# Query and key weights in halves, and later stores and loads, in the attention loop of a four-layer kernel on one core

## The chip, the core and the metric

The kernel runs on one core of a Trainium2 chip. The metric is the device time of one execution in microseconds (us). The core has five engines with a queue of instructions each: TensorE (PE, whose weight loads are the row PEld), VectorE (DVE), ScalarE (ACT), GpSimd (POOL) and SyncE (SP). In this kernel nearly all transfers between the chip's memory and the core's are issued on SP's queue, in the order in which they are written there; an instruction of SP that waits holds back everything behind it.

## The reference

`x` is 2048 rows of 512 numbers. Four layers follow each other, A, B, A, B, each added to its own input after a layer norm; this text is about B.

```
x = x + A(layernorm(x)); x = x + B(layernorm(x)); x = x + A(...); x = x + B(...)

B:  q, k, v = x @ wq, x @ wk, x @ wv      # 32 heads of 16, four segments of 512 rows
    for s in range(4):                     # M, z: memory, starts at zero
        p = softmax(q_s k_s^T / 4 + causal mask);   a_dot = p @ v_s
        a_mem = (phi(q_s) @ M) / (phi(q_s) @ z + 1e-6)      # phi(t) = t + 1 if t > 0 else exp(t)
        o_s = g * a_mem + (1 - g) * a_dot                   # g = sigmoid(beta), one for each head
        M += phi(k_s)^T v_s;  z += sum(phi(k_s))
    return o @ wo
```

A is a linear attention with a learned feature map (two softmaxes for each head), computed in two passes over the rows.

## The kernel before

All matrix products are made from high and low parts, `hi*hi + hi*lo + lo*hi`, so a weight or an activation is a pair of tiles (`hh` and `hl` for the normed rows, `oh` and `ol` for the attention's output).

The attention loop (`LayerB.steps`) runs once for each B layer, through 160 steps `k` and some ahead of them. A *segment* is 40 steps, a *period* five: the period works on four heads (two row halves of a group of eight). Step `k` = 40s + 5m + j is written as the cell "m.j" of a table; `FIRST` is the table of segment 0, `GAPS` of segments 1 and 2, `LAST` (first loop) and `FINAL` (second loop) of segment 3. In each step the attention proper comes first (`attend`: matmuls into `lg`, ACT's exponential into `P`; `maxima`: matmuls into `mx`, `my` or `g`, DVE's maxima; in a period's first step also `weighted`). Then come the functions that earlier steps put off to this step (`self.at`), the copies of projected K and Q into the attention's operand tiles (`stack`, the transfers `e<-ta`, three in step 2 and three in step 4 of a period), and last what the step's cell names, which fills PE's row between the attention's matmuls.

The cells that matter here:

- `Q0+/6` to `Q3/6`: six steps of `proj_pair`, the projection of query (m = 0) and key (m = 1) for a group of eight heads. The weights of a group are 512 KB for each of the two (a tile `wqk` of 128 rows, 2 parts x 4 row blocks x 128 columns), read from memory.
- `V+/6`: six steps of the values' projection of the next segment. `O/6`: six steps of `out_pair`, the output projection of two tiles of 128 rows of the segment before. Pair 1 runs in the cells 2.1 to 2.4, pair 2 in 3.1 to 3.4 (in `FINAL`, two half-width pairs each, 2.1 to 5.4).
- `turn`: transposes the attention's output of one row tile and loads the residual rows (`mmq<-x`, `xr<-x`).
- `load`: loads the four row tiles for a later segment's norm (`x<-x`). `n` runs a piece of that norm at the next step.
- `begin` in segment 2 starts the next layer's rows.

A pair (`mm3_pair`) has 24 steps of two matmuls each, which use 64 of PE's 128 rows each and start together. Sides change rows twice. In steps 0 to 5 the first side (the query's, for a projection) takes its row blocks 0 and 1 on the upper rows and the second side on the lower; in steps 6 to 17 all four row blocks are taken with the sides exchanged; in steps 18 to 23 the blocks 2 and 3 as at first. Step 6 and step 18 must follow the matmuls before them, which is written as a *handover*: a no-op on SP that waits for PE's last matmul, and PE's next that waits for the no-op. So four cells hold a pair (0 to 5, 6 to 11, 12 to 17, 18 to 23), and its two handovers stand in SP's queue at the ends of the first and third cell.

The refill (`queue_w`) of a pair's weights is asked for when the pair has ended: two transfers of 512 KB, into the tile that the pair has just read, each waiting for the pair's last matmul. Q2 (cells 0.1 to 0.4) is followed by Q3 (1.1 to 1.4) after one step; the other projections are a period apart. The first two projections of a loop (`proj`, before step 0) are made singly, without handovers.

`out_pair` ends, for each of its two row tiles, with ACT's copy, POOL's addition of the residual and the store on SP (`x<-xr`, `x<-mmq`), one after the other.

Each transfer on SP's queue waits, beside its data, for the landing of the transfer eight places ahead of it, since eight semaphores are used in turn.

Of the kernel before, what the change touches and what calls it, by code (L numbers as in the profile page):

```python
# [8 lines left out]
F32R = mybir.dt.float32r  # L9
# [6 lines left out]
D = 512  # L16
H = 32
DH = 16
P = 128
NSEG = 4  # L20
NC = D // P
# [35 lines left out]
1.0 t0 fin max     | 1.1 Q3/6          | 1.2 Q3/6          | 1.3 Q3/6 | 1.4 Q3/6  # L57
2.0 m0 ln ln ln ln max fin | 2.1 V+/6     | 2.2 V+/6 w        | 2.3 V+/6 | 2.4 V+/6 w
3.0 t1 fin max     | 3.1 V+/6          | 3.2 V+/6 w        | 3.3 V+/6 | 3.4 V+/6 w
4.0 m1 max fin     | 4.1 Q0+/6 load    | 4.2 Q0+/6         | 4.3 Q0+/6 | 4.4 Q0+/6  # L60
5.0 t2 fin max     | 5.1 V+/6          | 5.2 V+/6 n        | 5.3 V+/6 n | 5.4 V+/6
6.0 m2 t3 fin max  | 6.1 Q1+/6         | 6.2 Q1+/6 n       | 6.3 Q1+/6 n | 6.4 Q1+/6
7.0 m3 a0+ a0+ max fin | 7.1 V+/6      | 7.2 V+/6 n        | 7.3 V+/6 n | 7.4 V+/6
# [3 lines left out]
1.0 t0 turn fin max | 1.1 Q3/6      | 1.2 Q3/6 n        | 1.3 Q3/6 | 1.4 Q3/6  # L67
2.0 m0 turn t1 fin ln max | 2.1 O/6    | 2.2 O/6           | 2.3 O/6 | 2.4 O/6
3.0 m1 turn turn fin ln max | 3.1 O/6  | 3.2 O/6           | 3.3 O/6 | 3.4 O/6
4.0 ln ln a2 fin a2 max | 4.1 Q0+/6 load | 4.2 Q0+/6       | 4.3 Q0+/6 | 4.4 Q0+/6  # L70
5.0 t2 a3 fin max  | 5.1 V+/6 begin  | 5.2 V+/6 n N      | 5.3 V+/6 n N | 5.4 V+/6
6.0 m2 a3 t3 fin max | 6.1 Q1+/6       | 6.2 Q1+/6 n N     | 6.3 Q1+/6 n N | 6.4 Q1+/6
7.0 m3 a0+ a0+ max fin | 7.1 V+/6      | 7.2 V+/6 n N      | 7.3 V+/6 n N | 7.4 V+/6
# [26 lines left out]
@with_exitstack  # L100
def interleave_kernel(ctx, tc, x_in, a_wqkv, a_wphi, a_wo, b_wq, b_wk, b_wv, b_wo, b_beta,
                      c_ident, c_mask, c_bd, out):
    nc = tc.nc
    MUL, ADD, SUB, MAX, MIN = ALU.mult, ALU.add, ALU.subtract, ALU.max, ALU.min

    cp = ctx.enter_context(tc.tile_pool(name="cp", bufs=1))
    wp = ctx.enter_context(tc.tile_pool(name="wp", bufs=4))
# [7 lines left out]
    def nm(s):  # L115
        uid[0] += 1
        return f"{s}_{uid[0]}"

    def T2(tag, bufs, dt=F32, shape=(P, 512)):
        return sp.tile(list(shape), dt, tag=tag, bufs=bufs, name=nm(tag))  # L120

    def PS(tag, bufs, shape=(P, 512)):
        return ps.tile(list(shape), F32, tag=tag, bufs=bufs, name=nm(tag))
# [38 lines left out]
    dve, act, pool, sync = [Ordered(e) for e in (nc.vector, nc.scalar, nc.gpsimd, nc.sync)]  # L162
# [10 lines left out]
    def mm(*a, **k):  # L173
        n = a[0].free_size()
        work[0] += n / 2.26 if k["rhs"].dtype == F32R else (n * 2 / 2.4 + 25 if "tile_position" in k else 2 * max(112, n * 2 / 2.4))
        return held(nc.tensor.matmul(*a, **k))  # L176
# [5 lines left out]
    def dma(out, in_):  # L182
        sync.dma_start(out=out.bitcast(F32), in_=in_.bitcast(F32))
# [35 lines left out]
    def dtile(shape, name):  # L219
        return dr.tile(list(shape), F32, name=name)  # L220
# [10 lines left out]
    def bring(w, key, src=None, tag="w8", low=dve):  # L231
        hi, lo = wtiles(tag)
        w[:] = [hi, lo]
        if key in kept:
            for kc in range(NC):
                for t, k in zip((hi, lo), kept[key]):
                    dma(t[:, kc, :], k[:, kc, :])
                yield
            return
        for kc in range(NC):  # L240
            raw = src(kc)
            act.copy(hi[:, kc, :], raw)
            low.tensor_tensor(out=lo[:, kc, :], in0=raw, in1=hi[:, kc, :].bitcast(F32), op=SUB)
            yield
        kept[key] = (dtile((P, NC, D), key + "_hi"), dtile((P, NC, D), key + "_lo"))
        owed.extend(zip(kept[key], (hi, lo)))
# [48 lines left out]
    wqk = [dtile((P, NC, 2, NC, P), f"wqk{m}") for m in range(2)]  # L295
# [137 lines left out]
    def mm3(po, lhs, rhs, kcs=range(NC)):  # L433

        for kc in kcs:
            for n, (a, b) in enumerate(((0, 0), (0, 1), (1, 0))):
                mm(po, lhsT=lhs(a, kc), rhs=rhs(b, kc), start=(kc == kcs[0] and n == 0),
                   stop=(kc == kcs[-1] and n == 2))
            if kc < kcs[-1]:
                yield  # L440

    def after(i, j):

        tc.add_manual_dep(i.ins, j.ins.name,
                          mybir.DependencyInfo(mybir.DependencyClass.Sync, mybir.DependencyReason.DATA),
                          reason="the halves of the rows take turns at a bank")

    def mm3_pair(one, two, kcs=range(NC)):

        terms = [(kc, a, b) for kc in kcs for a, b in ((0, 0), (0, 1), (1, 0))]  # L450
        half = len(terms) // 2
        parts = [(terms[:half], (one, two)), (terms, (two, one)), (terms[half:], (one, two))]
        steps = [(*term, sides, n == 0) for part, sides in parts for n, term in enumerate(part)]
        for step, (kc, a, b, sides, first) in enumerate(steps):
            ends = step == 0, step == len(steps) - 1
            for row, (po, lhs, rhs) in zip((0, 64), sides):
                i = mm(po, lhsT=lhs(a, kc)[row : row + 64], rhs=rhs(b, kc)[row : row + 64],
                       start=ends[0], stop=ends[1], tile_position=(row, 0))
                if first and step > 0 and row == 0:
                    after(i, passed)  # L460
            if step + 1 < len(steps) and steps[step + 1][4]:
                passed = sync.nop(nofuse=True)
                after(passed, i)
            if not ends[1]:
                yield
# [33 lines left out]
        wait(end)  # L499
        yield  # L500

    def out_pair(tiles, xdst, w, w0=0, w1=D):

        pos = [PS("g", G) for _ in tiles]

        def side(po, o):
            return (po[:, 0 : w1 - w0], lambda a, kc: o[a][:, kc * P : (kc + 1) * P],
                    lambda b, kc: w[b][:, kc, w0:w1])

        yield from mm3_pair(*[side(po, o) for po, (x, i, o) in zip(pos, tiles)])  # L510
        for po, (x, i, o) in zip(pos, tiles):
            y = T2("tb3", TB3)[:, 0 : w1 - w0]
            act.copy(y, po[:, 0 : w1 - w0])
            pool.tensor_tensor(out=x[:, w0:w1], in0=y, in1=x[:, w0:w1], op=ADD)
            if w1 == D:
                sync.dma_start(out=xdst[i], in_=x)
        yield

    def weigh(out, p, eps, add, eng=pool):
# [451 lines left out]
    class LayerB:  # L971
# [24 lines left out]
            yield from v_tile(self.hT[s], self.wv, self.vv[s], ("g", G), (0, 3, 1, 2) if s == 0 else range(4),  # L996
                              2 if s == 1 else s > 0)

        def queue_w(self):

            if self.wnext:
                m, c = self.wnext.pop(0)
                w = wp.tile([P, 2, NC, P], F32R, tag="w4", bufs=2, name=nm("wqk"))
                dma(w, wqk[m][:, c])
                self.w4.append(w)

        def proj(self, s, c, m):

            d, hT, w = self.st.setdefault((s, c), {}), self.hT[s], self.w4.pop(0)
            pp = PS("g", G)  # L1010
            yield from mm3(pp, lambda a, kc: w[:, a, kc, :], lambda b, kc: hT[b][:, kc, :])
            self.queue_w()
            for n, f in enumerate(self.projected(s, c, m, pp)):
                self.at.setdefault(self.k + 1 + n, []).append(f)
            yield

        def proj_pair(self, s, c):

            self.st.setdefault((s, c), {})
            hT, ws = self.hT[s], [self.w4.pop(0) for _ in range(2)]  # L1020
            pps = [PS("g", G) for _ in range(2)]

            def side(pp, w):
                return pp, lambda a, kc: w[:, a, kc, :], lambda b, kc: hT[b][:, kc, :]

            yield from mm3_pair(*[side(pp, w) for pp, w in zip(pps, ws)])
            jobs = []
            for m in range(2):
                self.queue_w()
                jobs.append(self.projected(s, c, m, pps[m]))  # L1030
            for m, job in enumerate(jobs):
                for n, f in zip((2, 4, 6) if m == 0 else (3, 5), job):
                    self.at.setdefault(self.k + n, []).append(f)
            yield
# [211 lines left out]
        def out(self, s):  # L1246
            for t in (0, 2):
                tiles = [(x, 4 * s + t + n, oT) for n, (oT, x) in enumerate(self.turned[0:2])]
                del self.turned[0:2]
                parts = 2 if self.thin and s == NSEG - 2 else 1  # L1250
                for n in range(parts):
                    yield from out_pair(tiles, self.xdst, self.wo, n * D // parts, (n + 1) * D // parts)

        def early(self):

# [37 lines left out]
                sync.dma_start(out=self.xdst[4 * s + t], in_=self.xe[t])  # L1293

        def opening(self):
            self.w4 = []
            self.wnext = [(m, c) for _ in range(NSEG) for c in range(NC) for m in range(2)]
            for _ in range(2):
                self.queue_w()
                yield  # L1300
            self.wv = []
            yield from bring(self.wv, "bwv")
            self.norm0 = self.norm(0)
            next(self.norm0)
            fills = self.start()
            for n in (0, 0, 1, 0, 1, 0, 1, 1, 1, 1, 0, 1, 1, 1, 1, 1, 1, 1, 1):
                yield
                next(self.norm0 if n else fills, None)
# [150 lines left out]
    for i in range(2):  # L1459
# [3 lines left out]
        a2 = la[i].pass2()  # L1463
# [40 lines left out]
```

## Time and profile before

| | us |
|---|---|
| median of 3 runs (lowest to highest) | 1428.81 (1425.95 to 1428.88) |
| the profiled execution | 1426.99 |
| its span, from the first to the last instruction | 1425.3 |

The profile is of one execution. A row of the timeline reads: start, duration, engine, line, operation, what it writes `<-` what it reads, shape, number of equal instructions merged, and in brackets how long the engine had been idle before and what ended that. Engines with a "q" are the queue that issues transfers: a row there is the time of issuing, not of the transfer. Buffer numbers are left out, so `x<-xr` is a store of a residual tile. L154 is the line of a helper that records every instruction of DVE, ACT, POOL and SP, and L176 that of all matmuls; groups are told apart by their tiles. The first attention loop lies between 303 and 720 us, the second between 997 and 1410.

### The profile page before, as it was taken

Reading aid. Unit: us, or ns where it says so; the run is one execution under the profiler, and the core shown is the slowest. Engines: PE = TensorE matmul, PEld = TensorE weight load, DVE = VectorE, ACT = ScalarE, POOL = GpSimd, SP = SyncE. Lnnn points to the kernel's source line nnn. Section 1 sums busy time; section 2 is a strip of 40 time slices with the busy share of each in tenths; the row PEclk is TensorE's granted clock in tenths of the full one; section 3 lists DMA queues with packets and bytes.
Section 4 is the critical chain, followed back from the end, with each engine's and each line's share of the span. In section 5 each row is a group of like instructions: output and inputs, shape, how many; then the busy total and the mean of one; then the engine's idle time right before and its main releaser. Section 6 shows DMA issues by size and latency. Waiting matters only on the chain.

```text
span 1425.3 us, 36885 instructions
## 1 busy us (share of the span) xinstructions
PE 1350.1 (95%) x14136; PEld 1035.5 (73%) x14136; DVE 1051.4 (74%) x3261; ACT 809.3 (57%) x1198; POOL 688.9 (48%) x1052
## 2 busy tenths in 40 slices
PE   7999989999999999999899998999999999999987
PEld 6887778767677777777568886887766777777765
DVE  4665778677787887888646767867678878878872
ACT  5545345436677677676534434453566766766663
POOL 1568656414447447335324446542335556554441
PEclk9999999999999999999999999999999999999998
DMA  5397346535545445456431104754464554544431
GB/s 195 109 328 273 115 154 207 171 99 151 144 124 134 132 126 140 128 131 168 143 104 45 60 31 131 249 167 122 128 186 98 138 154 98 135 129 96 113 104 46
DMA packets 108800, 196.27 MB, mean 138 GB/s; under 512 B 14416, under 2 KB 27856, under 8 KB 107856
## 3 DMA queue, kind: packets, MB, share of 16 engines
q1 hardware_dynamic: 106656, 193.27, 46.4%
q8 instruction: 112, 1.84, 0.6%
q10 hardware_dynamic: 1968, 0.64, 0.2%
q14 instruction: 64, 0.52, 0.1%
HBM read 101.05 MB, written 39.85 MB: 99 GB/s over the span
## 4 chain that ended last, share of the span: by engine, by line
PE 64%; DVE 14%; ACT 6%; DMA 6%; POOL 5%; issue 3%; SPq 2%; ACTq 0%; DVEq 0%; POOLq 0%
PE g L176 49%; PE lg L176 6%; PE g L180 4%; ACT P L154 3%; DMA wqk<-wqk 3%; PE mx L176 3%; POOL tb L154 2%; DVE es L154 2%; POOL P L154 2%; SPq L154 2%; DVE g L154 1%; DVE my L154 1%; PE lg L180 1%; DVE mx L154 1%; PE my L176 1%
## 5 line engine op out<-in xcount | busy, mean ns | idle before, releaser
L154 ACT ACTIVATE P<-lg 128x1024 f32<-128x1024 f32 x320 | 329.4, 1029 | 183.1 <-PE lg L176 94.3
L154 POOL TENSOR_SCALAR_AFFINE_SELECT P<-P 128x256 f32<-128x256 f32 (+1 forms) x448 | 192.4, 444 | 337.2 <-ACT P L154 336.5
L176 PE MATMUL g<-hh,wqk 64*128 64x512 f32 (+1 forms) x960 | 193.8, 393 | 7.7 <-DMA wqk<-wqk 5.4
L154 DVE CUSTOM_DVE_ANT_0 mx<-mx,mask 128x128 f32<-128x128 f32 (+3 forms) x332 | 165.2, 498 | 34.9 <-PE my L176 28.2
L154 DVE CUSTOM_DVE_ANT_0 g<-g,mask 128x512 f32<-128x512 f32 x360 | 176.0, 545 | 15.8 <-PE g L176 15.1
L176 PE MATMUL g<-w,oh 64*128 64x512 f32 (+2 forms) x816 | 174.8, 390 | 5.4 <-SPq L154 3.7
L154 DVE CUSTOM_DVE_ANT_0 my<-my,mask 128x128 f32<-128x128 f32 (+3 forms) x332 | 172.3, 519 | 0.1
L176 PE MATMUL lg<-e,e 64*128 64x256 f32 (+2 forms) x1024 | 157.3, 354 | 15.2 <-ACT P L154 14.7
L176 PE MATMUL g<-P,v 128*32 128x512 f32 (+3 forms) x2048 | 151.1, 435 | 4.4 <-DVE mxs L154 4.0
L176 PE MATMUL g<-w,hh 64*128 64x512 f32 (+2 forms) x800 | 147.8, 359 | 3.1 <-ACT w L154 1.3
L154 DVE DVE_READ_ACCUMULATOR2_ANT mxs<- 128x1 f32 x1024 | 144.7, 141 | 0.0
L176 PEld LDWEIGHTS lg<-e,e 64*128 64x128 f32 x1024 | 95.5, 186 | 63.5 <-ACT P L154 41.1
L176 PEld LDWEIGHTS g<-hh,wqk 64*128 64x128 f32 (+1 forms) x960 | 114.3, 185 | 25.3 <-issue 5.3
L176 PEld LDWEIGHTS g<-P,v 128*32 128x32 f32 x2048 | 59.8, 109 | 89.0 <-issue 64.9
L154 POOL TENSOR_SCALAR tb<-tb 128x512 f32<-128x512 f32 x72 | 110.9, 1551 | 25.4 <-ACT tb L154 25.4
L176 PEld LDWEIGHTS g<-w,oh 64*128 64x128 f32 (+1 forms) x816 | 100.5, 190 | 27.3 <-SPq L154 8.6
L176 PE MATMUL g<-hl,wqk 64*128 64x512 f32 (+1 forms) x480 | 113.8, 391 | 0.4 <-DVE hl L154 0.4
L176 PE MATMUL g<-w,ol 64*128 64x512 f32 (+2 forms) x408 | 108.7, 382 | 0.5 <-DVE ol L154 0.5
L176 PEld LDWEIGHTS g<-w,hh 64*128 64x128 f32 (+1 forms) x800 | 93.4, 188 | 17.0 <-ACT w L154 1.6
L176 PE MATMUL g<-w,hl 64*128 64x512 f32 (+2 forms) x400 | 94.7, 357 | 0.0
L154 ACT COPY tb<-g 128x512 f32<-128x512 f32 (+1 forms) x124 | 66.8, 575 | 43.5 <-PE g L176 43.3
L176 PE MATMUL mx<-e,e 63*128 63x256 f32 (+2 forms) x332 | 88.9, 330 | 0.3 <-DVE mxs L154 0.2
(149 smaller groups left out, 2882.4 us busy)
## 6 DMA issues: line engine op xcount, KB each, us to landing
e<-ta SPq DMA_DIRECT2D x384, 128.0 KB
wqk<-wqk SPq DMA_DIRECT2D x64, 512.0 KB
x<-x SPq DMA_DIRECT2D x48, 256.0 KB
ot<-in SPq DMA_DIRECT2D x28, 256.0 KB
pq<-tb SPq DMA_DIRECT2D x24, 256.0 KB
tb<-pq SPq DMA_DIRECT2D x24, 256.0 KB
x<-xr SPq DMA_DIRECT2D x22, 256.0 KB
xr<-x SPq DMA_DIRECT2D x20, 256.0 KB
```

Of the source, the lines that this page charges most:

```text
L154: i = f(*a, **k)
L176: return held(nc.tensor.matmul(*a, **k))
L180: return held(nc.tensor.transpose(*a))
```

## The change

Three things.

1. The two weight tiles are allocated once, and a refill is made in halves: row blocks 0 and 1, and row blocks 2 and 3, of both the query's and the key's weights (256 KB each, in runs of 1 KB instead of 4 KB). In a pair, the first halves are asked for after step 12 has been written and the second halves after the last step. Single projections and the opening ask for both halves, one after the other.
2. The stores of an out pair are put off: by five steps in segments 1 and 2, by two in segment 3. In cell 3.4 (4.4) they then come behind the second handover of the pair that follows.
3. `load` moves from cell 4.1, where it followed the pair's first six steps, to 4.4, ahead of the last six.

The order on PE, DVE, ACT and POOL stays; SP's changes, with 64 transfers more.

```diff
-4.0 m1 max fin     | 4.1 Q0+/6 load    | 4.2 Q0+/6         | 4.3 Q0+/6 | 4.4 Q0+/6
+4.0 m1 max fin     | 4.1 Q0+/6         | 4.2 Q0+/6         | 4.3 Q0+/6 | 4.4 load Q0+/6
...
-4.0 ln ln a2 fin a2 max | 4.1 Q0+/6 load | 4.2 Q0+/6       | 4.3 Q0+/6 | 4.4 Q0+/6
+4.0 ln ln a2 fin a2 max | 4.1 Q0+/6      | 4.2 Q0+/6       | 4.3 Q0+/6 | 4.4 load Q0+/6
...
-    def out_pair(tiles, xdst, w, w0=0, w1=D):
+    def out_pair(tiles, xdst, w, soon, w0=0, w1=D):
...
             if w1 == D:
-                sync.dma_start(out=xdst[i], in_=x)
+                soon(lambda x=x, i=i: sync.dma_start(out=xdst[i], in_=x))
...
-        def queue_w(self):
-
-            if self.wnext:
-                m, c = self.wnext.pop(0)
-                w = wp.tile([P, 2, NC, P], F32R, tag="w4", bufs=2, name=nm("wqk"))
-                dma(w, wqk[m][:, c])
-                self.w4.append(w)
+        def queue_w(self, m, halves=range(2)):
+
+            for half in halves:
+                if self.wnext[m][half]:
+                    c, kcs = self.wnext[m][half].pop(0), slice(2 * half, 2 * half + 2)
+                    dma(self.w4[m][:, :, kcs, :], wqk[m][:, c, :, kcs, :])
...
-            yield from mm3_pair(*[side(pp, w) for pp, w in zip(pps, ws)])
+            for n, _ in enumerate(mm3_pair(*[side(pp, w) for pp, w in zip(pps, ws)])):
+                if n == 12:
+                    for m in range(2):
+                        self.queue_w(m, (0,))
+                yield
             jobs = []
             for m in range(2):
-                self.queue_w()
+                self.queue_w(m, (1,))
                 jobs.append(self.projected(s, c, m, pps[m]))
...
-                    yield from out_pair(tiles, self.xdst, self.wo, n * D // parts, (n + 1) * D // parts)
+                    yield from out_pair(tiles, self.xdst, self.wo, lambda f: self.at.setdefault(self.k + (5 if s < NSEG - 2 else 2), []).append(f),
+                                        n * D // parts, (n + 1) * D // parts)
...
-            self.w4 = []
-            self.wnext = [(m, c) for _ in range(NSEG) for c in range(NC) for m in range(2)]
-            for _ in range(2):
-                self.queue_w()
+            self.w4 = [wp.tile([P, 2, NC, P], F32R, tag="w4", bufs=2, name=nm("wqk")) for _ in range(2)]
+            self.wnext = [[[c for _ in range(NSEG) for c in range(NC)] for _ in range(2)] for _ in range(2)]
+            for m in range(2):
+                self.queue_w(m)
                 yield
```

More of the change, by code (lines that the diff above doesn't have):

```diff
@@ L997, in values @@
                               2 if s == 1 else s > 0)
-        def queue_w(self):
-            if self.wnext:
-                m, c = self.wnext.pop(0)
-                w = wp.tile([P, 2, NC, P], F32R, tag="w4", bufs=2, name=nm("wqk"))
-                dma(w, wqk[m][:, c])
-                self.w4.append(w)
+        def queue_w(self, m, halves=range(2)):
[3 more added lines that the diff above has]
+                    dma(self.w4[m][:, :, kcs, :], wqk[m][:, c, :, kcs, :])
         def proj(self, s, c, m):
-            d, hT, w = self.st.setdefault((s, c), {}), self.hT[s], self.w4.pop(0)
+            d, hT, w = self.st.setdefault((s, c), {}), self.hT[s], self.w4[m]
             pp = PS("g", G)
             yield from mm3(pp, lambda a, kc: w[:, a, kc, :], lambda b, kc: hT[b][:, kc, :])
-            self.queue_w()
+            self.queue_w(m)
             for n, f in enumerate(self.projected(s, c, m, pp)):
@@ L1019, in proj_pair @@
             self.st.setdefault((s, c), {})
-            hT, ws = self.hT[s], [self.w4.pop(0) for _ in range(2)]
+            hT, ws = self.hT[s], self.w4
             pps = [PS("g", G) for _ in range(2)]
@@ L1295, in opening @@
         def opening(self):
-            self.w4 = []
-            self.wnext = [(m, c) for _ in range(NSEG) for c in range(NC) for m in range(2)]
-            for _ in range(2):
-                self.queue_w()
+            self.w4 = [wp.tile([P, 2, NC, P], F32R, tag="w4", bufs=2, name=nm("wqk")) for _ in range(2)]
+            self.wnext = [[[c for _ in range(NSEG) for c in range(NC)] for _ in range(2)] for _ in range(2)]
+            for m in range(2):
+                self.queue_w(m)
                 yield
```

## The prediction

> **What bounds the kernel now.** I read the page first, then the waits of PE, then the timeline around the waits that the diff can touch.
>
> ```profile
> span 1425.3 us, 36885 instructions
> ...
> PE 1350.1 (95%) x14136; PEld 1035.5 (73%) x14136; DVE 1051.4 (74%) x3261; ACT 809.3 (57%) x1198; POOL 688.9 (48%) x1052
> ...
> PE 64%; DVE 14%; ACT 6%; DMA 6%; POOL 5%; issue 3%; SPq 2%; ACTq 0%; DVEq 0%; POOLq 0%
> ```
>
> PE is busy for 1350.1 of 1425.3 us and carries 64% of the chain that ended last. PE runs its instructions in one written order, which the change leaves as it is (only SP's order and the waits differ in the built program), so a gain is a gap in PE's row that closes, and a loss is one that opens. The waits, listed by who waited for whom (total us, times, longest), name the gaps:
>
> ```profile
> PE lg L176 <- ACT P L154: 14.7, 57, 0.6
> ...
> PE g L176 <- DMA wqk<-wqk: 5.4, 10, 0.8
> ...
> PE g L176 <- SPq L154: 4.4, 6, 1.1
> ```
>
> The second row is what the split refill is about, the third what the moved stores and loads are about: a handover goes through a no-op on SP's queue, so whatever SP is stuck on ahead of it holds PE.
>
> **The refill, as it is.** In segment 1 of the first attention loop SP issues both refills when the pair Q2 has ended; the chain of waits runs through the second:
>
> ```profile
> 418.69 1.01 SPq L154 DMA_DIRECT2D wqk<-wqk  x2
> ```
>
> ```profile
> 419.31 5.12 DMA wqk<-wqk
> ```
>
> Q3's first two matmuls, by PE's timeline:
>
> ```profile
> 423.41 0.39 PE L176 MATMUL g<-hh,wqk 64*128 64x512 f32 x1
> 424.57 0.47 PE L176 MATMUL g<-hh,wqk 64*128 64x512 f32 x1 [0.78 <-DMA wqk<-wqk]
> ```
>
> The query side's weights are there at 423.41, the key side's only at 424.4; the two matmuls of a step otherwise start together (x2 rows below). From start to start 1.16 us are lost, though the gap between the records is 0.78, because the first matmul's record runs 0.39 us and would have been overlapped. Where the first matmul of the pair is the one that waits, the surplus is smaller:
>
> ```profile
> 529.26 0.34 PE L176 MATMUL my<-e,e 63*128 63x384 f32 x1
> 529.87 0.47 PE L176 MATMUL g<-hh,wqk 64*128 64x512 f32 x1 [0.27 <-DMA wqk<-wqk]
> ...
> 470.62 0.33 PE L176 MATMUL my<-e,e 63*128 63x384 f32 x1
> 470.79 0.40 PE L176 MATMUL g<-hh,wqk 64*128 64x512 f32 x2
> 471.03 0.40 PE L176 MATMUL g<-hl,wqk 64*128 64x512 f32 x2
> ```
>
> That is 0.61 from start to start against 0.17 at an undisturbed place: 0.44 lost, 0.17 over the gap. Records overlap where PE runs undisturbed, so a stall has to be measured between starts: ten waits of 5.4 us in all cost 5.4 + 10 x 0.3 = 8.4 us (7.1 with 0.17 each, 9.2 with 0.38). [...]
>
> **What the halves do to it.** Half 0 (row blocks 0 and 1 of both weights) is queued after a pair's thirteenth step, when the last reader, step 11, may have ended; half 1 after the pair. Step 11's last matmuls, the thirteenth step and the nineteenth, which waits for the second handover, stand in the pair Q0+ of the same segment at 469.84, 470.79 (above) and 472.65:
>
> ```profile
> 466.60 0.54 PE L176 MATMUL g<-hh,wqk 64*128 64x512 f32 x2
> ...
> 469.84 0.40 PE L176 MATMUL g<-hh,wqk 64*128 64x512 f32 x2
> ...
> 472.65 0.40 PE L176 MATMUL g<-hh,wqk 64*128 64x512 f32 x2
> ```
>
> ```profile
> 474.53 1.05 SPq L154 DMA_DIRECT2D wqk<-wqk  x2
> ```
>
> Step 11 ends at 470.24, 4.3 us ahead of that pair's own refill. Q2's refill is issued at 418.69, so its half 0 can be issued near 414.4 and is due at 423.4, 9 us later; the whole 1 MB took 5.12 us, so half of it is there. Half 1 is issued at 418.7 as now and due at Q3's thirteenth step, 4.2 us (470.79 less 466.60, the pair's first step) after 423.4, thus 8.9 us again. Both fit, so the 8.4 us go and nothing of the refill comes last. Runs in the weights' rows shrink from 4 KB to 1 KB, bytes stay; should halves move at half the rate, 512 KB still need what 1 MB needs now, 5.12.
>
> **The stores, as they are.** The first out pair's stores wait for POOL's additions, which wait for ACT's copies; the next pair's residual loads and first handover stand behind them:
>
> ```profile
> 451.92 0.33 SPq L154 DMA_DIRECT2D x<-xr  x1
> 453.17 0.33 SPq L154 DMA_DIRECT2D x<-mmq  x1
> 453.54 0.43 SPq L154 DMA_DIRECT2D mmq<-x  x1
> 454.01 0.46 SPq L154 DMA_DIRECT2D xr<-x  x1
> ```
>
> ```profile
> 453.33 0.40 PE L176 MATMUL g<-e,e 63*128 63x512 f32 x2
> 454.87 0.73 PE L176 MATMUL g<-w,oh 64*128 64x512 f32 x4 [1.14 <-SPq L154]
> ...
> 561.11 0.50 PE L176 MATMUL g<-w,oh 64*128 64x512 f32 x2 [0.84 <-SPq L154]
> ...
> 1148.71 0.51 PE L176 MATMUL g<-w,oh 64*128 64x512 f32 x2 [0.86 <-SPq L154]
> ...
> 1255.29 0.50 PE L176 MATMUL g<-w,oh 64*128 64x512 f32 x2 [0.84 <-SPq L154]
> ```
>
> SP is free of the last load at 454.47 and PE goes on at 454.87. The four waits are 3.7 us by gaps; the start-to-start surplus is about 0.16 each (453.33 to 454.87 is 1.54, against the 0.24 that two such matmuls of 512 columns take, 470.79 to 471.03), so 4.3 us. With the stores five steps later, behind the second handover, the loads can be issued as soon as SP gets there, and the 4.3 go. The stores of the last out pairs move by two steps only, still ahead of a handover, where no row of PE shows a wait for SP now: nothing.
>
> **The next rows' loads.** Four loads at cell 4.1 hold the K and Q pieces and then the second handover of Q0+:
>
> ```profile
> 1162.25 2.46 SPq L154 DMA_DIRECT2D x<-x  x4
> ```
>
> ```profile
> 1166.70 0.50 PE L176 MATMUL g<-hh,wqk 64*128 64x512 f32 x2 [0.17 <-SPq L154]
> ```
>
> One such gap, 0.2 us. At 4.4 they stand ahead of the second halves, which are due a period later; their own reader (the first moments, at 5.3) comes four steps after, so nothing is lost there.
>
> **What it adds.** 64 more issues on SP:
>
> ```profile
> L154 SPq DMA_DIRECT2D wqk<-wqk x64: 319/405/656, 167.0 to 1325.2; - x64
> ...
> L154 SPq DMA_DIRECT2D wqk<-ta x16: 513/567/1448, 49.6 to 114.8; - x16
> ```
>
> Of these, 52 are inside pairs: 13 pairs in each loop have a first half to fetch, two issues each (16 head groups, less two projected singly and the last, with nothing to fetch). Two issues from 470.24 (step 11's end) take 0.8 us at the median, 1.1 at the 567 ns of the pieces with short runs, and the handover behind them is needed at 472.65: hidden, 2.4 us of cover. The other 12 (opening and single projections) lie in the second pass, where POOL sometimes waits for loads:
>
> ```profile
> POOL P L154 <- DMA tb<-pq: 11.9, 6, 2.8
> ```
>
> Between nothing and 12 x 0.405 = 4.9 us; SP mostly stands waiting there, so 0.6.
>
> **What stays of the gain.** Sum of the gaps: 8.4 + 4.3 + 0.2 = 12.9. Once PE is earlier, other engines can come last. Two rows of the windows view bound that (span, then PE, PEld, DVE, ACT, POOL busy, clock, DMA):
>
> ```profile
> 513.20:525.50 12.30, 12.30 (x133) 9.32 (x128) 10.31 (x42) 9.03 (x13) 8.90 (x17) 1.00 0.31 66
> 525.50:539.60 14.10, 13.05 (x133) 10.05 (x127) 10.24 (x38) 10.52 (x18) 5.73 (x10) 1.00 0.61 164
> ```
>
> ```profile
> ACT P L154 <- PE lg L176: 94.3, 121, 3.1
> ```
>
> The first stretch is Q2's period, the second Q3's, with two refill waits. Q2's runs in 12.3 us with DVE at 10.3; Q3's has 10.2 of DVE and 10.5 of ACT, so 12.3 to 12.4 is possible for it: all kept. Against that, ACT's lead where it stood waiting for PE is 94.3/121 = 0.78 us, less than the 1.16 that PE gains at a time: 0.78/1.16 = 67% kept. I take 80%: 10.3, less 0.6: 9.7 us. The profiled execution took 1426.99 around its span of 1425.3, so it would take 1417.3; the median of the runs is 1.8 above it, and 1428.8 - 9.7 = 1419.1.
>
> **Rivals.** (a) Part of it only. The residual loads (453.54, 454.01) may still come late ahead of the first handover, leaving 0.8 x 8.6 - 0.6 = 6.3 us, 1422.5; or the K pieces, now queued behind half 0 and the stores, come late for the maxima:
>
> ```profile
> 472.45 1.99 SPq L154 DMA_DIRECT2D e<-ta  x3
> ...
> 478.82 0.28 PE L176 MATMUL mx<-e,e 63*128 63x256 f32 x1
> ```
>
> With half 0 and the two stores, 1 MB, in front of them, counted from the K pieces' issue, near 473.1 by then, 5.12 us for it and 1.9 for their own 384 KB, they land at 480.1, 1.3 late, in four places: 5.2 us, and 1424.3 is left. Against it: half 0 is issued from 470.24 on, two microseconds before the stores. [...] (b) Nothing to measure: ACT's exponentials come last wherever PE is early; the 14.7 us of waits for them grow by what the others lose, about 1427. For it stands that 57 waits are there already, against it Q2's period. (c) Slower: the second handover comes late, because SP must issue two halves between step 11 and it. The cover is 2.4 us, so it decides from 1.2 us an issue, and outweighs the gain from (2.4 + 9.7/26)/2 = 1.39 us; at the 1.45 us of the slowest short-run piece above, 26 x 0.5 = 13 us come in, 1428.8 - 9.7 + 13 = 1432. The medians, 0.41 and 0.57, speak against it. (d) The halves are not independent, and PE waits at mid-pair for the half just asked for: 26 x 2.6 us (half of 5.12), 1493 with the stores' share of the gain. The built order shows the thirteenth step waiting for the earlier half alone, so I leave it at 1 in 100.
>
> **Chances.** Forecast 0.60, (a) 0.17, (b) 0.08, (c) 0.14, (d) 0.01. Some 0.2% (2.9 us) is what a measurement here tells from no change. Faster 0.77, same 0.08, slower 0.15. The range runs from all 12.9 kept and half of the 2.9 us between the lowest and the highest of the three runs (1414.4) to case (b), 1427.0.
>
> **What would show it.** Right: no wait of PE for the refill or, in the out pairs, for SP; the stretch from one Q2 to the next pair's end near 12.4; the half-0 issues ending before 472. Wrong: SPq gaps at the nineteenth step of pairs (c); the maxima waiting for K pieces at 5.1 (a); more and longer waits of PE for ACT's exponentials (b); a DMA gap at the thirteenth step (d).

## The result, and the profile after

| us | before | changed |
|---|---|---|
| median (lowest to highest), first measurement | 1428.85 (1425.95 to 1429.28), 4 runs | 1412.97 (1411.68 to 1415.26), 4 runs |
| ratio | | 0.9898 [0.9880, 0.9917] |
| median (lowest to highest), second measurement | 1428.46, 15 runs | 1415.22 (1412.31 to 1416.66), 6 runs |
| ratio | | 0.9911 [0.9893, 0.9929] |
| profiled execution, span | 1426.99, 1425.3 | 1415.26, 1413.5 |

The change makes the kernel faster by 13 to 16 us between the medians (the ratios give 14.6 and 12.7), where 9.7 were forecast; the first median lies 1.4 us under the low end of the range, the second inside it. First the page of the changed kernel (total, engines, shares of the chain, the costliest matmuls with their idle time, the DMA queue):

```profile
span 1413.5 us, 36969 instructions
...
PE 1347.8 (95%) x14136; PEld 1030.4 (73%) x14136; DVE 1047.4 (74%) x3261; ACT 809.7 (57%) x1198; POOL 689.3 (49%) x1052
...
q1 hardware_dynamic: 132256, 193.27, 46.8%
...
PE 70%; DVE 13%; ACT 6%; issue 4%; POOL 3%; DMA 2%; SPq 1%; ACTq 0%; DVEq 0%; POOLq 0%
...
L176 PE MATMUL g<-hh,wqk 64*128 64x512 f32 (+1 forms) x960 | 182.5, 392 | 2.0 <-ACT hh L154 1.4
```

The same rows of the page before:

```profile
q1 hardware_dynamic: 106656, 193.27, 46.4%
...
L176 PE MATMUL g<-hh,wqk 64*128 64x512 f32 (+1 forms) x960 | 193.8, 393 | 7.7 <-DMA wqk<-wqk 5.4
```

Work is the same on every engine; the chain loses 4 points of DMA and gains 6 of PE. The projections' idle time falls from 7.7 us, mostly for the refill, to 2.0, mostly for the normed rows at the start. The DMA queue moves the same 193.27 MB in a quarter more packets and occupies 46.8% of 1413.5 us, 661.5, against 46.4% of 1425.3, 661.3: the 1 KB runs cost the transfer engines nothing that these shares, rounded to 0.1% (1.4 us), could show.

PE's waits in the changed kernel (total, times, longest):

```profile
PE lg L176 <- ACT P L154: 14.2, 56, 0.6
...
PE g L176 <- SPq L154: 1.5, 3, 0.9
```

No row for the refill is left, SP's has fallen from 4.4 to 1.5, and the wait for the exponentials has not grown (14.7 before): nothing was given back there. Q3's first matmuls and the out pair's handover, by PE's timeline after:

```profile
424.47 0.39 PE L176 MATMUL g<-hh,wqk 64*128 64x512 f32 x2
...
453.35 0.40 PE L176 MATMUL g<-e,e 63*128 63x512 f32 x2
453.58 0.63 PE L176 MATMUL g<-w,oh 64*128 64x512 f32 x4
```

The two projections start together, as at an undisturbed place, and the out pair goes on 0.23 us after the maxima where it took 1.54. SP's timeline shows how early the first halves now are (four refills of 256 KB each, with the K and Q pieces between):

```profile
415.92 1.08 SPq L154 DMA_DIRECT2D wqk<-wqk  x2
417.82 1.81 SPq L154 DMA_DIRECT2D e<-ta  x3
419.74 1.05 SPq L154 DMA_DIRECT2D wqk<-wqk  x2
```

**Where the time came from.** ACT's first exponential of a period is a good mark. The two loops, from their first exponential to that of the last period (first loop) and of period 6 of segment 3 (second loop), in the timeline of ACT before:

```profile
303.49 1.03 ACT L154 ACTIVATE P<-lg 128x1024 f32<-128x1024 f32 x1 [3.14 <-PE lg L176]
...
708.52 1.01 ACT L154 ACTIVATE P<-lg 128x1024 f32<-128x1024 f32 x1
...
997.43 1.03 ACT L154 ACTIVATE P<-lg 128x1024 f32<-128x1024 f32 x1 [3.13 <-PE lg L176]
...
1384.35 1.03 ACT L154 ACTIVATE P<-lg 128x1024 f32<-128x1024 f32 x1
```

and after:

```profile
305.10 1.02 ACT L154 ACTIVATE P<-lg 128x1024 f32<-128x1024 f32 x1 [3.13 <-PE lg L176]
...
703.41 1.01 ACT L154 ACTIVATE P<-lg 128x1024 f32<-128x1024 f32 x1
...
993.22 1.03 ACT L154 ACTIVATE P<-lg 128x1024 f32<-128x1024 f32 x1 [3.12 <-PE lg L176]
...
1374.18 1.03 ACT L154 ACTIVATE P<-lg 128x1024 f32<-128x1024 f32 x1
```

405.0 + 386.9 = 791.9 us before, 398.3 + 381.0 = 779.3 after: 12.6 less. (The other stretches differ by +1.6 before the first loop, +0.9 between the loops and -1.6 behind the second, which add up to the 11.8 us between the spans. The last of these is not in the loop sum below: the period that starts at 1384.35 takes 15.53 us before, at a mean granted clock of 0.78, and the one that starts at 1374.18 takes 13.16 after, at 1.00; some 0.7 us are lost again behind it.) By the same marks, the eight periods of Q3 took 107.5 us before and 99.4 after, 8.1 less, and the four periods with a second out pair 58.7 and 54.0, 4.7 less. This *loop sum* is used for all runs below: it is from one profile of each kernel, but leaves out the ends of the kernel, where the profiles differ most even for the same opening (the first loop starts anywhere from 301.4 to 306.0 us in them). The changed kernel was profiled twice, and its loop sums are 0.4 us apart. Its second measurement had been expected to show 12 to 15 us less than before and a first loop of about 398.3 us; it showed 13.2 and 398.4.

### The profile page after: what moved, and what is told of

Same layout as the page of the kernel before. It is cut to its first block, busy times and chain, and to the rows that moved or that the text cites. A ratio compares the mean times of both kernels' runs of the same rounds, so it can differ in the third digit from the quotient of the medians.

```text
span 1413.5 us, 36969 instructions
## 1 busy us (share of the span) xinstructions
PE 1347.8 (95%) x14136; PEld 1030.4 (73%) x14136; DVE 1047.4 (74%) x3261; ACT 809.7 (57%) x1198; POOL 689.3 (49%) x1052
## 3 DMA queue, kind: packets, MB, share of 16 engines
q1 hardware_dynamic: 132256, 193.27, 46.8%
## 4 chain that ended last, share of the span: by engine, by line
PE 70%; DVE 13%; ACT 6%; issue 4%; POOL 3%; DMA 2%; SPq 1%; ACTq 0%; DVEq 0%; POOLq 0%
PE g L176 53%; PE lg L176 6%; PE g L180 5%; PE mx L176 3%; ACT P L154 3%; DVE es L154 2%; POOL P L154 1%; PE lg L180 1%; DVE g L154 1%; DVE my L154 1%; DVE mx L154 1%; ACT U L154 1%; PE my L176 1%; DVE mxs L154 1%; DVE ol L154 1%
## 5 line engine op out<-in xcount | busy, mean ns | idle before, releaser
L154 DVE CUSTOM_DVE_ANT_0 g<-g,mask 128x512 f32<-128x512 f32 x360 | 176.2, 545 | 14.2 <-PE g L176 13.7
L176 PE MATMUL g<-hh,wqk 64*128 64x512 f32 (+1 forms) x960 | 182.5, 392 | 2.0 <-ACT hh L154 1.4
L176 PE MATMUL lg<-e,e 64*128 64x256 f32 (+2 forms) x1024 | 153.0, 354 | 14.7 <-ACT P L154 14.2
L176 PEld LDWEIGHTS lg<-e,e 64*128 64x128 f32 x1024 | 91.3, 185 | 65.5 <-ACT P L154 42.5
L176 PEld LDWEIGHTS g<-hh,wqk 64*128 64x128 f32 (+1 forms) x960 | 100.8, 185 | 19.3 <-ACT hh L154 1.8
L176 PE MATMUL g<-w,ol 64*128 64x512 f32 (+2 forms) x408 | 108.4, 379 | 0.5 <-DVE ol L154 0.5
L176 PE MATMUL g<-hl,wqk 64*128 64x512 f32 (+1 forms) x480 | 103.6, 390 | 0.4 <-DVE hl L154 0.4
```

Of the source, the lines that this page charges most:

```text
L154: i = f(*a, **k)
```

## The experiments

Each edit is shown against the changed kernel unless it says otherwise. Times of before are those of the same chip and hour, so they differ a little from run to run of the study.

**The halves alone.** Stores and loads as before.

```diff
-4.0 m1 max fin     | 4.1 Q0+/6         | 4.2 Q0+/6         | 4.3 Q0+/6 | 4.4 load Q0+/6
+4.0 m1 max fin     | 4.1 Q0+/6 load    | 4.2 Q0+/6         | 4.3 Q0+/6 | 4.4 Q0+/6
...
-  lambda f: self.at.setdefault(self.k + (5 if s < NSEG - 2 else 2), []).append(f)
+  lambda f: f()
```

> The refill in halves alone; stores and next rows' loads stand where they were. Theory 1 (gaps add up and nothing is given back): the refill's waits go, eleven in all with the one that the trace books under ACT, 8.4 + 0.7 us between starts, so about 1419.5 us; the four SP waits of the second out pair stay at 0.84 to 1.14 us. Theory 2 (a fifth of what PE gains comes back as waits for ACT, as the prediction had it): 6.7 us, 1422, and PE's waits for ACT's exponentials grow by 1 to 2 us. Theory 3 (most of the gain over the forecast is TensorE's half-clock stretches lying elsewhere): the attention loops shorten as in theory 1 or 2, but the median moves by another 2 us or more either way with no gap to show for it.

Measured: 1425.17 us (12 runs) beside 1427.67; ratio 0.9981 [0.9969, 0.9994], loop sum 789.8. The refill waits are gone, and yet only 2.1 us of the loops. PE's waits, and the worst place on SP's timeline and on PE's:

```profile
PE g L176 <- SPq L154: 8.9, 10, 1.8
```

```profile
1162.33 1.75 SPq L154 DMA_DIRECT2D x<-x  x4
1164.13 1.83 SPq L154 DMA_DIRECT2D e<-ta  x3
1166.05 2.25 SPq L154 DMA_DIRECT2D wqk<-wqk  x2
```

```profile
1166.20 0.43 PE L176 MATMUL g<-e,e 63*128 63x256 f32 x4
1168.42 0.50 PE L176 MATMUL g<-hh,wqk 64*128 64x512 f32 x2 [1.79 <-SPq L154]
```

With the four row loads still at 4.1, SP issues without a pause from 1162.33: loads, three K and Q pieces, two halves, and only then the no-op for which Q0+'s nineteenth step waits. The waits stand in Q0+ of segments 0 and 1 of both loops (0.68, 0.67, 1.46 and 1.79 us). Those four periods took 59.5 us against 53.4 before, 6.1 more, which is what the halves had gained, less 2.

**Stores and loads alone.** The refill whole, as before; the other two parts of the change kept.

```diff
-        def queue_w(self, m, halves=range(2)):
+        def queue_w(self):
...
-            for n, _ in enumerate(mm3_pair(...)):
-                if n == 12:
-                    for m in range(2):
-                        self.queue_w(m, (0,))
-                yield
+            yield from mm3_pair(...)
```

> The later stores and loads alone; the refill is whole, at the pair's end. Theory 1: the four SP waits go, 4.3 us between starts, and the one at the nineteenth step 0.2, so about 1424.3; the refill waits of 5.4 us by gaps stay. Theory 2: 3.6 us, 1425.2. Theory 3: as theory 1 or 2 and 2 us or more either way.

Measured: 1424.02 us (12 runs) beside 1427.67; 0.9981 [0.9968, 0.9994], loop sum 788.5, so 3.5 less than before. The refill stays:

```profile
PE g L176 <- DMA wqk<-wqk: 5.3, 7, 0.8
```

The out pairs' periods take 13.50 us, as in the changed kernel. The halves alone and these two parts alone bring 2.1 and 3.5 us of the loops; together they bring 12.6. The 7.0 us that exist only when both are there are found by the periods: the 6.1 that the halves alone lose in Q0+, and 0.9 in Q3, whose eight periods take 108.4 us here against 107.5 before.

**The loads back to 4.1, all else of the change kept.** Both tables that have the cell are changed; one is shown.

```diff
-4.0 m1 max fin     | 4.1 Q0+/6         | 4.2 Q0+/6         | 4.3 Q0+/6 | 4.4 load Q0+/6
+4.0 m1 max fin     | 4.1 Q0+/6 load    | 4.2 Q0+/6         | 4.3 Q0+/6 | 4.4 Q0+/6
```

> The change with the next rows' loads back in cell 4.1, all else as changed. Theory 1 (gaps simply add, each part worth its own): 0.2 us lost, 1413. Theory 2, from the halves-only run: four loads of some 0.4 us, three K or Q pieces and two first halves then stand between the two handovers of Q0+, more than PE's time there, so the nineteenth step waits in segments 0 and 1 of both loops: 0.96 + 0.9 + 1.7 + 2.6 = about 6 us lost in period 4, so 1419.

Measured: 1420.02 us (10 runs) beside 1428.46; 0.9946 [0.9930, 0.9962], loop sum 783.8, 4.5 more than the changed kernel.

```profile
PE g L176 <- SPq L154: 5.4, 5, 1.9
```

The waits are at the same four nineteenth steps (0.69, 1.31, 1.25, 1.86). Moving the loads is worth some 4 us once the halves are there. Without the halves, in the experiment before this one, the four periods with these waits are only 0.5 us shorter than before the change.

**The stores back, all else of the change kept.**

```diff
-  lambda f: self.at.setdefault(self.k + (5 if s < NSEG - 2 else 2), []).append(f)
+  lambda f: f()
```

> The change with the stores of an out pair issued at once again, all else as changed. Both theories: the four waits of the second out pair's first handover come back, 4.3 us by the prediction and 4.7 by the two profiles, so about 1417.5; no new wait at the nineteenth step of Q0+, since period 4 of segment 2, which has no loads, was no longer in the halves-only run than before.

Measured: 1416.79 us (6 runs) beside 1428.46; 0.9928 [0.9911, 0.9945], loop sum 784.5, 5.2 more than the changed kernel. The four waits of the out pairs are back, 0.84 to 0.87 us each; the first of them, at its old place, had been 1.14:

```profile
454.69 0.73 PE L176 MATMUL g<-w,oh 64*128 64x512 f32 x4 [0.85 <-SPq L154]
```

By the out pairs' four periods alone the stores are worth 4.4 us. Stores and loads are independent of each other to within 1 us: 4.5 and 5.2 added to 779.3 give 789.0, and the kernel with the halves alone, which has neither, stands at 789.8.

**The halves alone, but the first ones behind the second handover.** The first experiment with one number changed, so that SP has the same issues and bytes, in another order.

```diff
-                if n == 12:
+                if n == 18:
```

> The halves-only kernel (stores and loads where they were) with the first halves asked for after the nineteenth step, behind the second handover. If SP's queue is why halves alone gave little (loads, pieces and halves all between the two handovers of Q0+), the waits at the nineteenth step go and halves alone give 8 us, 1420, with the four store waits still there. If the loads' and the halves' bytes stand in each other's way, the place in the queue changes little: 1424 to 1425 as before.

Measured: 1420.17 us (6 runs) beside 1428.61; 0.9943 [0.9928, 0.9958], loop sum 784.3, so 5.6 less than with the halves at step 12. At the place shown above:

```profile
1154.68 1.75 SPq L154 DMA_DIRECT2D x<-x  x4
1156.48 4.68 SPq L154 DMA_DIRECT2D e<-ta  x6
1161.26 1.08 SPq L154 DMA_DIRECT2D wqk<-wqk  x2
```

and in PE's waits:

```profile
PE g L176 <- SPq L154: 3.7, 6, 0.9
...
PE g L176 <- DMA wqk<-wqk: 0.8, 3, 0.3
```

The 3.7 us are the stores' four old waits (0.82 to 0.85), one of 0.15 at a nineteenth step and one of 0.19 in the next layer. The four Q0+ periods take 53.4 us, as before the change. What took the gain of the halves alone is thus the two issues' place in SP's queue between the two handovers, not their number or their bytes.

**Both halves asked for when the pair has ended**, first halves of both weights first.

```diff
-                if n == 12:
-                    for m in range(2):
-                        self.queue_w(m, (0,))
...
+            for half in range(2):
+                for m in range(2):
+                    self.queue_w(m, (half,))
             for m in range(2):
-                self.queue_w(m, (1,))
```

> All of the change, but both halves are asked for when the pair has ended, first halves of both weights ahead of the second halves. If the early asking in mid-pair carries the refill's gain, the waits stay: first halves land some 1.3 us earlier than the whole did, so that what is left is a third of 8.4 or less, 3 us, near 1416. If it is enough that Q3 starts on halves (the whole was only 1.2 us late, and half the bytes are ahead of the first steps), nothing is left and the time is that of the change, 1413. If halving costs by itself (a fixed cost for each transfer), the waits are as before or longer, 1421 or more.

Measured: 1414.47 us (6 runs) beside 1427.67; 0.9911 [0.9897, 0.9926], loop sum 779.2: the same as the whole change within what can be told.

```profile
PE g L176 <- DMA wqk<-wqk: 0.9, 4, 0.3
```

Asking in the middle of the pair saves these 0.9 us and pays with two more waits for SP (of 0.34 and 0.28); nearly all of the refill's gain comes from the halves in this order, since a pair needs only 512 KB to start and the second 512 KB twelve steps (two cells) later. The prediction had put the gain down to the earlier asking.

**More issues in the same place.** The first halves in eight transfers of 64 KB instead of two of 256 KB, to take the cover of the second handover away.

```diff
+                    for kc in (2 * half, 2 * half + 1):
+                        for a in ((slice(0, 2),) if pieces == 2 else (slice(0, 1), slice(1, 2))):
+                            dma(self.w4[m][:, a, kc, :], wqk[m][:, c, a, kc, :])
...
-                        self.queue_w(m, (0,))
+                        self.queue_w(m, (0,), 4)
```

> The change with the first halves in eight transfers of 64 KB (runs of 512 bytes) instead of two of 256 KB, all at the same place in mid-pair. By the cover of 2.4 us between step 11 and the second handover, eight issues of some 0.55 us are 4.4 us, so each of 26 second handovers comes 2.0 us late: 52 us more, 1465, with SP waits of about 2 us at the nineteenth step of every such pair. If SP's place is no limit (issues overlap, or the handover does not stand behind them), 1413 to 1416.

Measured: 1485.25 us (4 runs) beside 1427.67; 1.0412 [1.0396, 1.0427].

```profile
PE g L176 <- SPq L154: 52.8, 27, 3.4
```

```profile
483.20 1.81 SPq L154 DMA_DIRECT2D e<-ta  x3
485.11 3.87 SPq L154 DMA_DIRECT2D wqk<-wqk  x8
```

```profile
487.33 0.40 PE L176 MATMUL g<-e,e 63*128 63x256 f32 x4
489.09 0.50 PE L176 MATMUL g<-hh,wqk 64*128 64x512 f32 x2 [1.37 <-SPq L154]
```

SP issues until 488.98 and PE goes on at 489.09. This is rival (c) of the prediction brought about by the edit. The time is 20 us beyond the expectation although the gaps came as expected; the section on the hardware returns to that.

**Four issues of 128 KB** (`self.queue_w(m, (0,), 2)` in the edit above).

> The change with the first halves in four transfers of 128 KB instead of two of 256 KB, at the same place in mid-pair. Between the two handovers SP issues three K or Q pieces (1.8 us) and these four; PE takes 4.5 us from the first handover's step to the nineteenth. At 0.45 us each four take 1.8 us: 3.6 us, 0.9 us of room, so 1413 to 1418 and waits only where a single issue is stretched. If the handover's cost starts with any issue more (no room), half of the 72 us of eight issues: 1450.

Measured: 1421.79 us (6 runs) beside 1428.61; 0.9951 [0.9932, 0.9970], loop sum 787.3.

```profile
PE g L176 <- SPq L154: 6.0, 8, 1.4
```

That is 8 us of the loops lost by two more issues at each place, where 1413 to 1418 us had been expected. Four such issues take 2.11 us in SP's timeline at 468.36, and most pairs show no wait; at the largest of the waits, 1.37 us at 1058.77, they took 3.52. So four still fit when nothing holds SP up, with little to spare, and two leave room for all but the slowest.

**First halves and the next layer's row loads behind their handovers.** The three waits for SP that the changed kernel still has are two first halves whose issue took long and, at 678.12, a handover of the next layer's values queued behind that layer's row loads. Both are moved by one place.

```diff
-                for _ in range(5):
+                for _ in range(6):
...
-                for _ in range(3):
+                for _ in range(2):
...
-                if n == 12:
+                if n == 18:
```

> The change with the first halves asked for after the nineteenth step, so behind the second handover too, and in the next layer's values the row loads one call later, behind their second handover. If a first half that takes long to issue is what made PE wait at two nineteenth steps (0.34 and 0.28 us by gaps) and row loads what made it wait in the values (0.89), these three go: 1.5 us, 1411.5, and Q3 still starts without a wait since the halves asked for at the pair's end already did so nearly everywhere. If the first halves come late instead, up to 2 us of refill waits are back, 1413 to 1415.

Measured: 1413.19 us (6 runs) beside 1428.46; 0.9897 [0.9879, 0.9914], loop sum 778.0. The three waits are gone; 0.4 us of refill are back in two places, and one wait for SP of 0.35 us stands in the values' projection, at 342.60. Beside the changed kernel on the same chip (1415.22, lowest 1412.31, highest 1416.66; this one 1409.22 to 1415.75) that is 2 us less, and by the loop sums 1.3 to 1.7; the intervals overlap, so that it is faster than the change isn't shown.

| loop sum, us | |
|---|---|
| before | 791.9 |
| halves alone, at step 12 | 789.8 |
| stores and loads alone | 788.5 |
| halves alone, first ones behind the handover | 784.3 |
| change without the stores | 784.5 |
| change without the loads | 783.8 |
| change | 779.3; 779.6 in a second profile |
| change, all halves at the pair's end | 779.2 |
| change, first halves and row loads behind the handovers | 778.0 |
| change, four issues in mid-pair | 787.3 |
| change, eight issues in mid-pair | 851.7 |

## Why the prediction was right and where it was wrong

**The refill: right, the size in part by luck.** It gave 8.4 us from ten waits of 5.4, by measuring starts and not gaps; Q3's periods give 8.1. But 1.0 of that is an eleventh wait, which the prediction didn't count: in segment 3 of the first loop PE's row has 0.69 us at 636.52 that the trace puts down to ACT's exponentials, and it goes with the others. Nine of the ten stand in the other seven periods of Q3, which give 7.1, so 0.2 us over each gap and not 0.3; the tenth, of 0.17 us, stands at 266.29, before the first loop. Gaps alone would have said 5.4. Measuring from start to start thus led the right way. That the refill would be early enough held with much room: even asked for at the pair's end, by halves, it costs only 0.9.

**The fear of small transfers: unfounded.** The prediction allowed for halves that move at half the rate, an assumption that no trace of before could test. The queue's time with 64 wholes and with 128 halves, 661.3 and 661.5 us, shows no such price here.

**The stores: right.** 4.3 predicted, 4.7 by the out pairs' periods, 4.4 when they alone are put back.

**The loads: mis-sized.** 0.2 was the wait that stood in the trace before. Their worth with the halves in place is 4.5, and that had to be worked out from the queue as it would be, not from the waits as they were. The sum came out right all the same, since these 4.5 us are a loss avoided and no gain. That is luck: by the prediction's own terms the loads could have stayed at 4.1 for 0.2 us.

**The cover of the second handover: right, as long as nothing stands ahead of the K and Q pieces.** The prediction took 2.4 us, from step 11's end to the nineteenth step, for two issues, and didn't mention the three pieces that SP also issues between the two handovers. SP's timeline in the changed kernel, in the first loop,

```profile
620.97 1.81 SPq L154 DMA_DIRECT2D e<-ta  x3
622.87 2.49 SPq L154 DMA_DIRECT2D wqk<-wqk  x2
```

and PE's, with step 11's last matmuls and the nineteenth step:

```profile
622.31 0.40 PE L176 MATMUL g<-hh,wqk 64*128 64x512 f32 x2
...
625.48 0.50 PE L176 MATMUL g<-hh,wqk 64*128 64x512 f32 x2 [0.34 <-SPq L154]
```

The pieces end at 622.78 and step 11 at 622.71, so they take nothing of the cover, and the nineteenth step could have come at 625.14, 2.4 us later. Two issues take 1.1 of it as a rule; PE waits here because these two took 2.49. With the four loads ahead of them the pieces end late: in the kernel with the halves alone at 1165.96, by the rows shown there, where step 11 ends at 1164.17. That is what the prediction left out, and why the loads' 0.2 was mis-sized.

Rival (c) needed 1.2 us an issue at every pair and is not seen; slow issues cost 0.34 and 0.28 us at two places. With the loads left at 4.1, the waits at the nineteenth steps cost 4.5 us, not the whole gain. Rivals (a), (b) and (d) are not seen: no K piece comes late for the maxima, the waits for the exponentials are 14.2 us where they were 14.7, and the thirteenth steps wait for nothing.

**What stays of the gain: the step that failed.** The sum of gaps was 12.9, and 12.6 came out of the loops, 98%. The prediction kept 80% of it, 10.3, between all (Q2's period) and 67% (ACT's mean lead of 0.78 us over 121 waits); this term is 2.3 us too small. The mean was the wrong row: where PE stood waiting for the refill, ACT stood waiting for PE as well, for longer. ACT's timeline at Q3 of segment 2 before,

```profile
529.81 1.02 ACT L154 ACTIVATE P<-lg 128x1024 f32<-128x1024 f32 x1 [0.64 <-PE my L176]
533.13 1.03 ACT L154 ACTIVATE P<-lg 128x1024 f32<-128x1024 f32 x1 [1.79 <-PE g L176]
```

and after:

```profile
528.34 1.03 ACT L154 ACTIVATE P<-lg 128x1024 f32<-128x1024 f32 x1 [0.64 <-PE my L176]
530.09 1.03 ACT L154 ACTIVATE P<-lg 128x1024 f32<-128x1024 f32 x1 [0.21 <-PE lg L176]
```

ACT had 1.79 us idle at that very place, and 1.58 of it go: the 3.32 us between the two starts become 1.75, which is the whole of what the period gains (14.02 to 12.45). It is the same at all twelve places, eight of Q3 and four of the out pairs: ACT stood waiting there for 0.80 to 2.32 us before, and still for 0.21 to 0.90 after. The two stretches that the prediction compared, Q2's and Q3's, by the windows view after (span, then PE, PEld, DVE, ACT, POOL busy, clock, DMA):

```profile
511.80:524.10 12.30, 12.30 (x132) 9.30 (x125) 10.33 (x42) 9.07 (x14) 8.85 (x17) 1.00 0.45 114
524.10:536.55 12.45, 12.45 (x129) 8.92 (x125) 9.74 (x38) 10.44 (x18) 5.72 (x10) 1.00 0.61 171
```

Q3 runs at 12.45, as the argument from Q2 had it (12.3 to 12.4), with PE busy throughout. Had that argument been followed, the forecast would have been 1428.8 - 12.9 + 0.6 = 1416.5, 3.5 above the first measured median and 1.3 above the second.

**The 0.6 us for extra issues in the second pass** could not be seen, and no run shows it: the stretch from the start to the first loop, where those of the first B layer lie, differs by 1.6 us between the two profiles, but kernels with the same opening start their first loop at 301.4 (halves alone behind the handover) to 306.0 us (both halves at the end).

**The range** reached down to all 12.9 kept and 1.5 us for the runs, and the first median lies below it. The intervals of the two ratios stand for 11.9 to 17.1 us and 10.1 to 15.3, so that 12.6 lies in both. What the two profiles have beyond the loops is the 1.6 us behind the second loop. No gap closes there (PE is idle for 8.5 us of that stretch in both); PE's granted clock over it is 0.87 before and 0.91 after, and the prediction had no term for that. Whether it belongs to the change is open: nine of the eleven profiles of kernels with the change or parts of it have the period there at 13.1 to 13.2 us, but the halves alone have it at 14.1, and with the first ones behind the handover at 15.6, as before.

## What to carry to other kernels

Whether an engine off the path can follow is read at the stalls that go, in its own row there, and not from its mean lead over the kernel. A queue of transfers that also carries handovers has to be laid out anew for a change: count everything issued between two handovers, also what stays, for an edit that removes 0.2 us of waiting today may be what another edit's 4 us depend on. And when a tile is refilled behind its reader, the order of its parts can be worth more than the time of asking.

## What the runs showed of the hardware that was not expected

**PE's clock after short gaps.** The kernel with eight issues lost 20 us more than its gaps: its loop sum is 72.4 us above the changed kernel's, its waits for SP 51.3. The windows view of it, around a gap of 2.86 us that ends at 544.28 (span, PE, PEld, DVE, ACT, POOL, clock, DMA):

```profile
541.90:545.30 3.40, 1.02 (x8) 0.86 (x10) 1.19 (x7) 1.04 (x2) 0.64 (x1) 1.00 0.35 93
545.30:548.70 3.40, 3.40 (x18) 1.31 (x18) 1.41 (x4) 2.00 (x3) 0.30 (x1) 0.52 0.86 200
```

and of the kernel with the halves alone, around the gap of 1.79 us that ends at 1168.42:

```profile
1164.90:1168.31 3.41, 1.73 (x20) 1.44 (x16) 3.18 (x16) 1.72 (x2) 1.40 (x3) 1.00 0.89 248
1168.31:1171.72 3.41, 3.30 (x16) 2.22 (x16) 0.00 (x0) 0.67 (x2) 0.00 (x0) 0.58 0.96 286
```

In both, the granted clock is 1.00 over a stretch of 3.4 us in which PE is busy for 1.02 or 1.73 us, and 0.52 or 0.58 over the next. The loops of the kernel with eight issues hold ten such stretches, those of the changed kernel none (1.00 over both loops); the mean granted clock of the whole execution is 0.982 and 0.994. Half of ten times 3.4 us is 17 us, and 0.16 us from start to start at each of the 24 more waits is another 4: as an estimate, that is the 21 us. The two stretches shown stand behind gaps of 2.86 and 1.79 us. Behind a gap of 1.86 us in the change without the loads, which ends at 1164.66, no such stretch shows: two matmuls of 512 columns take 0.39 us in PE's timeline up to 1165.92, as ahead of the gap, and the mean granted clock of that execution is 0.995. Nor does a gap alone decide it elsewhere: in the kernel before, PE is busy for 2.02 of the 3.40 us up to 1390.50, and the clock is 0.50 over the next 3.40; in the changed kernel, with the same matmuls there, for 2.04 of the 3.40 us up to 1380.35, and the clock stays at 1.00 over the next 3.40. What decides it besides the gap is not shown by these runs.

**Single issues on SP.** Of the 52 issues of two refills of 256 KB each in the changed kernel's loops, 46 take 0.88 to 1.09 us of SP's queue, three 1.14 to 1.43 and three 2.10 to 2.49 (the row at 622.87 is one); the one at 1166.05 in the kernel with the halves alone takes 2.25. What holds them is not visible in the traces and was not tried.
